# Four sizes of each expert projection, chosen at run time, in a linear-attention and hash-routing kernel

## The chip, the cores and the metric

The kernel runs on one core of one Trainium2 chip. The metric is the device time of one execution in microseconds (us). TensorE multiplies matrices, VectorE and ScalarE work on elements, GpSimd starts the gathers and scatters with indices, SyncE starts plain transfers.

## The reference

Linear attention with decay over 4 sequences of 768 positions and 8 heads of 64, and then a layer of experts: each of the 3,072 tokens goes to one of 8 experts by a hash of its id.

```python
expert_idx = token_ids * np.int64(2654435761) % np.int64(E)      # E = 8
for e in range(E):
    mask = expert_idx == e
    xe = x[mask]                          # x: [3072, 512], the attention's output
    h = np.maximum(xe @ w1[e], 0.0)       # w1[e]: [512, 1024]
    out[mask] = h @ w2[e]                 # w2[e]: [1024, 512]
```

All of it is in float32. The ids are random but fixed by a seed; the kernel doesn't know them when it is built, and computes the routing on the chip.

## The kernel before

It goes through 24 units of attention, each 128 positions of one sequence. Between them it computes the routing on VectorE: experts are ranked by their count of tokens, and the expert of rank w gets "window" w, with room for `CAPS[w]` tokens. Tokens that don't fit go to a loop at the end. The rows of a window are gathered, transposed, projected twice and scattered.

```python
EARLY = 19
CAPS = [376, 384, 392, 392, 400, 408, 416, 432]
PACE = 1400
ORDER = [0, 2, 3, 4, 5, 6, 7, 1]
...
        cap = route.tile([P, E], F32)          # capacity of each expert's window
...
        nc.vector.tensor_tensor(ee, iota_s[:, 0:E].unsqueeze(2).to_broadcast([P, E, E]),
                                win.unsqueeze(1).to_broadcast([P, E, E]), op=OP.is_equal)
        nc.vector.tensor_mul(ee, ee, iota_s[:, 0:E].unsqueeze(1).to_broadcast([P, E, E]))
        nc.vector.tensor_reduce(who_i[:], ee, axis=AX.X, op=OP.add)
...
        key_e = route.tile([P, E, NC], F32)    # tokens beyond the capacity are moved to the end
        nc.vector.tensor_tensor(key_e[:], cum, cap[:].unsqueeze(2).to_broadcast([P, E, NC]), op=OP.is_ge)
```

`yield n` in the routing says how much VectorE work a step is; after each attention unit, steps worth `PACE` are let through.

The projections of all but the first one use a scheme of seven products instead of eight for a 2x2 block matrix. The tokens of a window are split into two halves, the inner dimension and the outputs too. Sums of blocks are made on VectorE beforehand, and products are combined afterwards:

```python
    def quarters(x):
        K, M = x.shape[1] // 2, x.shape[2] // 2
        return [[x[:, j * K:(j + 1) * K, i * M:(i + 1) * M] for j in range(2)] for i in range(2)]

    def token_sums(x, name):
        a = quarters(x)
        ...
        todo = [lambda: nc.vector.tensor_add(s1, a[1][0], a[1][1]), lambda: nc.vector.tensor_sub(s2, s1, a[0][0]),
                lambda: nc.vector.tensor_sub(s3, a[0][0], a[1][0]), lambda: nc.vector.tensor_sub(s4, a[0][1], s2)]
        return [None, a[0][0], a[0][1], s4, a[1][1], s1, s2, s3], todo

    def seven(a, b, c, g, relu, todo):
        K, T = a[1].shape[1], a[1].shape[2]          # T: tokens of one half
        def product(i):
            ...
            for m in range(2):
                at = (2 * g + m) * P
                for k in range(K):
                    nc.tensor.matmul(ps[:, m, :], b[i][:, k, at:at + P], a[i][:, k, :],
                                     start=k == 0, stop=k == K - 1)          # L658
```

A first projection calls `seven` twice (K = 2), a second one once (K = 4), so each has 7 x 2 x 4 = 56 matmuls. A float32 matmul is two weight loads and two matmuls in the records, so a projection has 112 of each. The loop over the windows:

```python
    for n, e in enumerate(ORDER):
        then = ORDER[n + 1] if n + 1 < E else None
        ...
        if n == 0:
            flush(todo)
            eight(xTs[e], w1s[e], hT)                # the plain form, L718
        else:
            past = ORDER[n - 1]
            ...
            part = squares(past) // 2
            (both0, others0, _), (both1, others1, _) = (seven(a1, b1, quarters(hT[:]), g, True, todo) for g in range(2))
            others0(both0())
            turn_out(past, 0, part)                  # transpose and scatter of the window before
            others1(both1())
            turn_out(past, part, squares(past))
        a2, sums2 = token_sums(hT[:], f"h_{e}")
        ...
        flush(sums2)
        b1, todo = weight_sums(w1s[then], f"w1_{then}")
        todo.insert(2, lambda: turn(0, squares(then)))
        a1, more = token_sums(xTs[then], f"x_{then}")
        both, others, _ = seven(a2, b2, quarters(yT[:, :, 0:CAPS[e]]), 0, False, todo)
        others(both())
        flush(todo + more)
```

The only branches of the program are those of the loop over overflow tiles at the end.

Of the kernel before, what the change touches and what calls it, by code (L numbers as in the profile page):

```python
# [7 lines left out]
F32 = mybir.dt.float32  # L8
BF16 = mybir.dt.bfloat16
I32 = mybir.dt.int32  # L10
# [6 lines left out]
EARLY = 19  # L17
FIRST = 288

CAPS = [376, 384, 392, 392, 400, 408, 416, 432]  # L20
WBUFS = 3
UBUFS = 2
WARM = 10
PACE = 1400
W_AT = [20, 21, 22, 23]
ORDER = [0, 2, 3, 4, 5, 6, 7, 1]
SQ = 32
PACE_FIRST = 500

# [2 lines left out]
def kernel(  # L32
# [189 lines left out]
    q_dec = aconst.tile([P, HP, C], F32)  # L222
    ident = const.tile([P, P], F32)
    who_i = route.tile([P, E], I32)
    oend = route.tile([P, E], F32)
    ntot_i = route.tile([P, 1], I32)
    idx_all = route.tile([P, NTILE], I32)
# [32 lines left out]
    def routing():  # L260
# [48 lines left out]
        nc.vector.tensor_reduce(cap[:], ee, axis=AX.X, op=OP.add)  # L309
        yield 250  # L310

        nc.vector.tensor_tensor(ee, iota_s[:, 0:E].unsqueeze(2).to_broadcast([P, E, E]),
                                win.unsqueeze(1).to_broadcast([P, E, E]), op=OP.is_equal)
        yield 250
        nc.vector.tensor_mul(ee, ee, iota_s[:, 0:E].unsqueeze(1).to_broadcast([P, E, E]))
        yield 250
        with nc.allow_low_precision("sums of one number each, below 8"):
            nc.vector.tensor_reduce(who_i[:], ee, axis=AX.X, op=OP.add)
# [12 lines left out]

        nc.vector.tensor_add(cnt, cnt, gap[:])
        yield 200
        nc.vector.tensor_sub(cnt, cnt, cap[:])
        yield 200
        och_i = route.tile([P, E], I32)
# [22 lines left out]
        nc.vector.tensor_sub(shift, shift, cap[:])  # L359
        yield 200  # L360

        key_e = route.tile([P, E, NC], F32)
        nc.vector.tensor_tensor(key_e[:], cum, cap[:].unsqueeze(2).to_broadcast([P, E, NC]), op=OP.is_ge)
        yield 400
        nc.vector.tensor_mul(key_e[:], key_e[:], shift.unsqueeze(2).to_broadcast([P, E, NC]))
# [54 lines left out]
        nc.vector.tensor_scalar(x_rows[:].rearrange("p t k -> p k t"), list_ps[:], piece[:, 1:2], None, op0=OP.add)  # L420
        done.append("lists")
        yield 400

        b_i = route.tile([P, NTILE], I32)
        nc.vector.tensor_scalar(b_i[:], rc[:, 1], -1.0, None, op0=OP.add)
# [119 lines left out]

    w1s, w2s = {}, {}
    first_src = []

    def load_first(i):
        for part, at in enumerate(W_AT):  # L550
# [14 lines left out]
    for i, u in enumerate(units):  # L565
        if i + AHEAD < len(units):
            loads[units[i + AHEAD]] = load_qkv(*units[i + AHEAD])
        if i > 0:
            store_x(i - 1)
        if i == B:  # L570
            for b in range(0, NB, NB // 2):
                nc.sync.dma_start(
                    x_dram[0:DP * P, :].rearrange("(p b) q -> p b q", p=P)[:, b:b + NB // 2, :],
                    zeros[:].bitcast(F32).rearrange("p (b q) -> p b q", q=P))
        load_first(i)
        if i == 0:
            attention(*u, *ready.pop(u))
        if i + 1 < len(units):
            ready[units[i + 1]] = scores(*units[i + 1])
        if i > 0:  # L580
            attention(*u, *ready.pop(u))
        room = PACE if i >= B else PACE_FIRST
        while room > 0:
            room -= next(todo, TURN)
        if i >= EARLY:
            assert "lists" in done
            if i == EARLY:
                xT, gathers, turn = gather_window(0)
                xTs = {0: xT[:, :, 0:CAPS[0]]}
                early = gathers[:FIRST // SQ]  # L590
                del gathers[:FIRST // SQ]
            for _ in range(3):
                if early:
                    early.pop(0)()
            if i == len(units) - 2:
                turn(0, NB)
# [28 lines left out]
        return ([None, b[0][0], b[1][0], b[1][1], t4, t1, t2, t3],  # L625
                [lambda x=x: nc.vector.tensor_sub(*x) for x in todo])  # L626

    def quarters(x):
        K, M = x.shape[1] // 2, x.shape[2] // 2
        return [[x[:, j * K:(j + 1) * K, i * M:(i + 1) * M] for j in range(2)] for i in range(2)]  # L630

    def token_sums(x, name):
        a = quarters(x)
        K, M = x.shape[1] // 2, x.shape[2] // 2
        s = sums.tile([P, 3, K, M], F32, tag=f"s{K}", name=f"{name}_s")
        s1, s2, s4 = (s[:, i] for i in range(3))
        s3 = a[1][0]
        todo = [lambda: nc.vector.tensor_add(s1, a[1][0], a[1][1]), lambda: nc.vector.tensor_sub(s2, s1, a[0][0]),
                lambda: nc.vector.tensor_sub(s3, a[0][0], a[1][0]), lambda: nc.vector.tensor_sub(s4, a[0][1], s2)]  # L639
        return [None, a[0][0], a[0][1], s4, a[1][1], s1, s2, s3], todo  # L640

    def flush(todo):
        while todo:
            todo.pop(0)()

    def seven(a, b, c, g, relu, todo):

        K, T = a[1].shape[1], a[1].shape[2]  # L650

        def product(i):
            ps = psC.tile([P, 2, T], F32, tag="c", name=f"p{i}") if i in (5, 7) else psA.tile(
                [P, 2, T], F32, tag="a", name=f"p{i}")
# [5 lines that stand above are left out]
            return ps  # L660

        def one_more():
            if todo:
                todo.pop(0)()

        def done(i, j, ps, u):
            o = c[i][j][:, 2 * g:2 * g + 2, :]
            nc.vector.tensor_add(o, ps[:], u[:])  # L668
            if relu:
                nc.scalar.activation(o, o, AF.Relu)  # L670

        def both():

            u1 = sums.tile([P, 2, T], F32, tag="u1", bufs=UBUFS, name="u1")
            nc.scalar.copy(u1[:], product(1)[:])  # L675
            done(0, 0, product(2), u1)
            return u1

        def others(u1):
            u2, u3 = (sums.tile([P, 2, T], F32, tag=f"u{i}", bufs=UBUFS, name=f"u{i}") for i in (2, 3))  # L680
            p7 = product(7)
            one_more()
            p5 = product(5)
            one_more()
            if len(todo) > 2:
                one_more()
            nc.vector.tensor_add(u2[:], product(6)[:], u1[:])  # L687
            nc.vector.tensor_add(u3[:], p7[:], u2[:])
            done(1, 1, p5, u3)
            nc.vector.tensor_add(u2[:], p5[:], u2[:])  # L690
            one_more()
            done(1, 0, product(4), u3)
            one_more()
            done(0, 1, product(3), u2)

        def last(u1, then):

            u2, u3 = (sums.tile([P, 2, T], F32, tag=f"u{i}", bufs=UBUFS, name=f"u{i}") for i in (2, 3))
            p5 = product(5)
            nc.vector.tensor_add(u2[:], product(6)[:], u1[:])  # L700
            nc.vector.tensor_add(u3[:], p5[:], u2[:])
            done(0, 1, product(3), u3)
            nc.vector.tensor_add(u2[:], product(7)[:], u2[:])
            then()
            done(1, 1, p5, u2)
            done(1, 0, product(4), u2)

        return both, others, last
# [50 lines left out]
    def squares(e):  # L759
        return -(-CAPS[e] // SQ)  # L760
# [10 lines left out]
    for n, e in enumerate(ORDER):  # L771
        then = ORDER[n + 1] if n + 1 < E else None
        hT = sums.tile([P, FP, CAPS[e]], F32, tag="hT", name=f"hT_{e}")
        b2, todo = weight_sums(w2s[e], f"w2_{e}")
        if then is not None:
            xT, gathers, turn = gather_window(then)
            xTs[then] = xT[:, :, 0:CAPS[then]]
            flush(gathers)
        if n == 0:
            flush(todo)  # L780
            eight(xTs[e], w1s[e], hT)
        else:
            past = ORDER[n - 1]
            if then is None:

                nc.gpsimd.drain()
            part = squares(past) // 2
            (both0, others0, _), (both1, others1, _) = (seven(a1, b1, quarters(hT[:]), g, True, todo) for g in range(2))
            others0(both0())
            turn_out(past, 0, part)  # L790
            others1(both1())
            turn_out(past, part, squares(past))
        a2, sums2 = token_sums(hT[:], f"h_{e}")
        if then is None:
            flush(sums2)
            both, _, last = seven(a2, b2, quarters(yT[:, :, 0:CAPS[e]]), 0, False, [])
            whole = CAPS[e] // 2 // P
            last(both(), lambda: rows(e, range(whole)))
            rows(e, range(whole, NT))
            continue  # L800
        if then not in w1s:
            w1s[then] = load_window_w1(then)
        w2s[then] = load_window_w2(then)
        flush(sums2)
        b1, todo = weight_sums(w1s[then], f"w1_{then}")
        todo.insert(2, lambda: turn(0, squares(then)))
        a1, more = token_sums(xTs[then], f"x_{then}")
        both, others, _ = seven(a2, b2, quarters(yT[:, :, 0:CAPS[e]]), 0, False, todo)
        others(both())
        flush(todo + more)  # L810
    order.close()

    def overflow_tile(w1, w2, xT):
# [97 lines left out]
```

## Time and profile before

| | |
|---|---|
| time, median of 3 | 423.95 us (423.4 to 425.21) |
| span of the profiled execution | 516.1 us, mean TensorE clock 0.901 |
| TensorE busy (matmul, weight load) | 436.5 us, 406.4 us |
| VectorE, ScalarE, GpSimd busy | 308.5, 67.9, 259.0 us |
| moved by the DMA engines | 78.92 MB, mean 153 GB/s |

The profiled execution is slower than the timed ones. In the profile, PE is TensorE's matrix array and PEld its weight loads, DVE is VectorE, ACT ScalarE, POOL GpSimd and SP SyncE. PEclk is the clock that TensorE was granted, as a share of full speed or, in the rows of slices, in tenths of it. Lines of the kernel are written L658 for line 658. `<-` stands for "written from", and after "idle" it names what ended a wait. "issue" is idle time for which the profile shows no cause. Queue 8 and queue 14 of the DMA engines carry instructions.

### The profile page before, as it was taken

What the parts mean: (1) busy time and instruction counts of PE and PEld (TensorE: products, weight loads), DVE (VectorE), ACT (ScalarE), POOL (GpSimd) and SP (SyncE); (2) the same over time, 40 slices, a digit from 0 to 9 for tenths busy, and PEclk for the clock granted to TensorE, in tenths of its full rate; (3) what the DMA queues carried; (4) which work ended last, traced back from release to release, by engine and by line L of the source; (5) the groups of instructions that cost most, each with busy time, mean ns of one, the idle gap of its engine ahead of it and who ended that gap; (6) DMA issues with size and microseconds to landing.
All of it is one profiled execution on the core that took longest, in us unless ns stands there. A gap on an engine that the chain in (4) does not pass through costs nothing. (4 is left out here: it accounts for less than half of the span.)

```text
span 516.1 us, 8543 instructions
## 1 busy us (share of the span) xinstructions
PE 436.5 (85%) x3349; PEld 406.4 (79%) x3349; DVE 308.5 (60%) x492; ACT 67.9 (13%) x166; POOL 259.0 (50%) x266
## 2 busy tenths in 40 slices
PE   7998989779539999999839966999489948999993
PEld 4787878669429999999729935999389938999982
DVE  7887886534004777779346533774477437768821
ACT  1022332001001021021001100120012001201200
POOL 5454654437760018767752772067706760650552
PEclk9898999979757999999969955999879987999997
DMA  8899899975214035246141610424153414230011
GB/s 311 307 402 328 279 339 314 311 259 178 82 51 161 16 156 201 81 162 210 46 143 67 213 44 25 164 90 151 46 174 89 152 46 163 78 150 1 32 34 62
DMA packets 28105, 78.92 MB, mean 153 GB/s; under 512 B 4521, under 2 KB 6829, under 8 KB 25120
## 3 DMA queue, kind: packets, MB, share of 16 engines
q1 hardware_dynamic: 18160, 59.01, 32.5%
q0 software_dynamic: 6448, 13.06, 8.2%
q10 hardware_dynamic: 3456, 6.29, 3.3%
q8 instruction: 27, 0.44, 0.3%
q14 instruction: 14, 0.11, 0.1%
HBM read 65.50 MB, written 13.30 MB: 153 GB/s over the span
## 5 line engine op out<-in xcount | busy, mean ns | idle before, releaser
L753 POOL DMA_INDIRECT out_dram<-o_by,out_rows x91 | 100.1, 1100 | 157.0 <-DVE o_by L749 131.7
L538 POOL DMA_INDIRECT g<-x_pieces,x_rows x91 | 96.4, 1059 | 27.7 <-issue 26.2
L658 PE MATMUL p<-xT,w 128*128 128x196 f32 (+5 forms) x336 | 67.4, 352 | 29.7 <-DVE xT L639 22.8
L658 PEld LDWEIGHTS p<-xT,w 128*128 128x128 f32 x336 | 60.7, 200 | 33.7 <-DVE xT L639 24.7
L658 PE MATMUL p<-hT,w 128*128 128x196 f32 (+6 forms) x384 | 67.7, 336 | 0.1
L658 PEld LDWEIGHTS p<-hT,w 128*128 128x128 f32 x384 | 66.3, 193 | 0.3 <-issue 0.3
L658 PE MATMUL p<-h_s,w_t 128*128 128x196 f32 (+6 forms) x256 | 51.0, 349 | 6.8 <-issue 6.8
L658 PEld LDWEIGHTS p<-h_s,w_t 128*128 128x128 f32 x256 | 45.2, 198 | 11.2 <-issue 11.2
L687 DVE TENSOR_TENSOR u<-p,u 128x392 f32<-128x392 f32 (+6 forms) x21 | 12.1, 578 | 63.4 <-PE p L658 45.3
L668 DVE TENSOR_TENSOR yT<-p,u 128x392 f32<-128x392 f32 (+6 forms) x32 | 18.4, 574 | 51.0 <-remote 39.6
L718 PE MATMUL ps<-xT,w 128*128 128x128 f32 (+1 forms) x192 | 32.7, 319 | 16.3 <-issue 16.0
L718 PEld LDWEIGHTS ps<-xT,w 128*128 128x128 f32 x192 | 29.4, 228 | 19.6 <-issue 19.4
L670 ACT ACTIVATE hT<-hT 128x392 f32<-128x392 f32 (+5 forms) x56 | 30.1, 540 | 97.5 <-DVE hT L668 91.6
L658 PE MATMUL p<-x_s,w_t 128*128 128x196 f32 (+5 forms) x224 | 41.5, 339 | 0.0
L658 PEld LDWEIGHTS p<-x_s,w_t 128*128 128x128 f32 x224 | 39.9, 196 | 0.1
L626 DVE TENSOR_TENSOR w_t<-w,w_t 128x1024 f32<-128x1024 f32 x30 | 36.5, 1218 | 0.0
L675 ACT COPY u<-p 128x392 f32<-128x392 f32 (+6 forms) x22 | 10.7, 488 | 193.7 <-PE p L658 98.2
L473 DVE TENSOR_TENSOR sm<-sps,decay 128x512 f32<-128x512 f32 x48 | 30.8, 682 | 8.6 <-remote 4.3
L479 POOL TENSOR_TENSOR qd<-qkv,q_dec 128x512 f32<-128x512 f32 x17 | 21.6, 1271 | 26.7 <-DMA qkv<-in_qkv_dram 22.6
L467 PE MATMUL sps<-qkv 64*128 64x128 f32 x384 | 28.0, 285 | 7.6 <-DMA qkv<-in_qkv_dram 7.6
L668 DVE TENSOR_TENSOR hT<-p,u 128x392 f32<-128x392 f32 (+5 forms) x56 | 31.9, 575 | 4.2 <-ACT u L675 1.6
L467 PEld LDWEIGHTS sps<-qkv 64*128 64x128 f32 x384 | 23.4, 188 | 12.1 <-DMA qkv<-in_qkv_dram 9.1
(150 smaller groups left out, 585.1 us busy)
## 6 DMA issues: line engine op xcount, KB each, us to landing
w<-in_moe_w_dram SPq DMA_DIRECT2D x15, 2048.0 KB
qkv<-in_qkv_dram SPq DMA_DIRECT2D x23, 1024.0 KB
x_pieces<-turned ACTq DMA_DIRECT2D x24, 256.0 KB
w<-in_moe_w_dram SPq DMA_DIRECT2D x4, 512.0 KB
g<-x_pieces,x_rows POOLq DMA_INDIRECT x91
out_dram<-o_by,out_rows POOLq DMA_INDIRECT x91
qkv<-in_qkv_dram SPq DMA_DIRECT2D x2, 512.0 KB
x_pieces<-zeros SPq DMA_DIRECT2D x2, 128.0 KB
```

The source lines that it names most:

```text
L467: nc.tensor.matmul(sps[hd][:, hp, :], kT[half[hd], hp, :], qT[half[hd], hp, :], start=True, stop=True)
L473: nc.vector.tensor_mul(sm[:, hd], sps[hd][:], decay[:, hd])
L479: eng.tensor_tensor(qd[:], qT, q_dec[:], op=OP.mult)
L538: nc.gpsimd.indirect_dma_start(out=dst, out_offset=None, in_=x_dram[0:rows, :], in_offset=bass.IndirectOffsetOnAxis(ap=idx, axis=0), bound ...
L626: [lambda x=x: nc.vector.tensor_sub(*x) for x in todo])
L658: nc.tensor.matmul(ps[:, m, :], b[i][:, k, at:at + P], a[i][:, k, :], start=k == 0, stop=k == K - 1)
L668: nc.vector.tensor_add(o, ps[:], u[:])
L670: nc.scalar.activation(o, o, AF.Relu)
L675: nc.scalar.copy(u1[:], product(1)[:])
L687: nc.vector.tensor_add(u2[:], product(6)[:], u1[:])
L718: nc.tensor.matmul(ps[:, m, :], w[:, k, (f + m) * P:(f + m + 1) * P], x[:, k, ts], start=k == 0, stop=k == DP - 1)
L753: st = nc.gpsimd.indirect_dma_start(out=out_pieces, out_offset=bass.IndirectOffsetOnAxis(ap=out_rows[:, e * NT + t, k:k + 1], axis=0), in_ ...
```

## The change

For each of the windows 1 to 7 both projections are there four times, for half sizes of `CAPS/2`, `CAPS/2 - 4`, `CAPS/2 - 8` and `CAPS/2 - 12` tokens. All engines branch to the smallest that holds the expert's tokens. For this the tokens are dealt evenly to both halves: those from the middle of the expert's own count on are moved to the start of the second half. The aim is that TensorE doesn't multiply columns that hold no token. Window 0 keeps its one size.

```diff
-PACE = 1400
+PACE = 1500
+ARMS, STEP = 4, 4
+    arm_i = route.tile([P, E], I32)
...
+        size = route.tile([P, E], I32)
+        nc.vector.tensor_scalar(size[:], cnt, 1.0, None, op0=OP.add)
+        nc.vector.tensor_scalar(size[:], size[:], 1, None, op0=OP.logical_shift_right)
+        half_n = route.tile([P, E], F32)
+        nc.vector.scalar_tensor_tensor(half_n[:], cap[:], 0.5, size[:], op0=OP.mult, op1=OP.min)
+        move = route.tile([P, E], F32)
+        nc.gpsimd.tensor_scalar(move[:], cap[:], 0.5, None, op0=OP.mult)
+        nc.gpsimd.tensor_sub(move[:], move[:], half_n[:])
+        other = route.tile([P, E], F32)
+        nc.gpsimd.tensor_scalar(other[:], first[:], 0.0, None, op0=OP.is_equal)
+        nc.gpsimd.tensor_mul(move[:], move[:], other[:])
+        arm = route.tile([P, E], F32)
+        nc.gpsimd.tensor_scalar(arm[:], move[:], float((ARMS - 1) * STEP), None, op0=OP.min)
...
+        nc.vector.tensor_tensor(key_e[:], cum, half_n[:].unsqueeze(2).to_broadcast([P, E, NC]), op=OP.is_ge)
+        nc.vector.tensor_mul(key_e[:], key_e[:], move[:].unsqueeze(2).to_broadcast([P, E, NC]))
+        nc.vector.tensor_add(cum, cum, key_e[:])
...
+        nc.vector.tensor_mul(ee, by_win[:], arm[:].unsqueeze(1).to_broadcast([P, E, E]))
+        nc.vector.tensor_reduce(arm_i[:], ee, axis=AX.X, op=OP.add)
+        nc.vector.tensor_scalar(arm_i[:], arm_i[:], STEP.bit_length() - 1, None, op0=OP.logical_shift_right)
...
+        if i == EARLY + 1:
+            _, arms = nc.values_load_multi_w_load_instructions(
+                arm_i[0:1, :], min_val=0, max_val=ARMS - 1, ...)
+            arm_of.extend(arms)
...
-    def quarters(x):
+    def quarters(x, n=None):
         K, M = x.shape[1] // 2, x.shape[2] // 2
-        return [[x[:, j * K:(j + 1) * K, i * M:(i + 1) * M] for j in range(2)] for i in range(2)]
+        return [[x[:, j * K:(j + 1) * K, i * M:i * M + (n or M)] for j in range(2)] for i in range(2)]
+    def by_size(w, body):
+        def among(lo, hi):
+            if hi - lo == 1:
+                body(CAPS[w] // 2 - STEP * lo)
+                return
+            mid = (lo + hi) // 2
+            with tc.If(arm_of[w] < mid) as less:
+                among(lo, mid)
+            with less.Else():
+                among(mid, hi)
+        among(0, ARMS)
...
-            (both0, others0, _), (both1, others1, _) = (seven(a1, b1, quarters(hT[:]), g, True, todo) for g in range(2))
-            others0(both0())
-            turn_out(past, 0, part)
-            others1(both1())
-            turn_out(past, part, squares(past))
+            def up(size):
+                rest = list(todo)
+                (both0, others0, _), (both1, others1, _) = (
+                    seven(some(a1, size), b1, quarters(hT[:], size), g, True, rest) for g in range(2))
+                others0(both0())
+                turn_out(past, 0, part)
+                others1(both1())
+                turn_out(past, part, squares(past))
+            by_size(e, up)
...
-        both, others, _ = seven(a2, b2, quarters(yT[:, :, 0:CAPS[e]]), 0, False, todo)
-        others(both())
-        flush(todo + more)
+        def down(size):
+            flush(sums2(size))
+            rest = todo + more()
+            both, others, _ = seven(some(a2, size), b2, quarters(yT[:, :, 0:CAPS[e]], size), 0, False, rest)
+            others(both())
+            flush(rest)
+        if n == 0:
+            down(CAPS[e] // 2)
+        else:
+            by_size(e, down)
```

`some(a, n)` cuts all operands to n tokens, and `token_sums` now makes its sums for n tokens. The second projection of the last window has the four sizes in the same way. The four arms stand one after the other in each engine's program; an arm begins behind two compares with a branch, and ends with a jump to behind the last arm. TensorE's part of one arm is 112 weight loads, 112 matmuls and some four more instructions.

More of the change, by code (lines that the diff above doesn't have):

```diff
@@ L310, in routing @@
         yield 250
-        nc.vector.tensor_tensor(ee, iota_s[:, 0:E].unsqueeze(2).to_broadcast([P, E, E]),
+        by_win = route.tile([P, E, E], F32)
+        nc.vector.tensor_tensor(by_win[:], iota_s[:, 0:E].unsqueeze(2).to_broadcast([P, E, E]),
                                 win.unsqueeze(1).to_broadcast([P, E, E]), op=OP.is_equal)
         yield 250
-        nc.vector.tensor_mul(ee, ee, iota_s[:, 0:E].unsqueeze(1).to_broadcast([P, E, E]))
+        nc.vector.tensor_mul(ee, by_win[:], iota_s[:, 0:E].unsqueeze(1).to_broadcast([P, E, E]))
         yield 250
@@ L333, in routing @@
         yield 200
+        size = route.tile([P, E], I32)
+        nc.vector.tensor_scalar(size[:], cnt, 1.0, None, op0=OP.add)
+        yield 200
+        nc.vector.tensor_scalar(size[:], size[:], 1, None, op0=OP.logical_shift_right)
+        yield 200
+        half_n = route.tile([P, E], F32)
[6 more added lines that the diff above has]
+        nc.gpsimd.tensor_mul(move[:], move[:], other[:])
+        yield 400
+        arm = route.tile([P, E], F32)
+        nc.gpsimd.tensor_scalar(arm[:], move[:], float((ARMS - 1) * STEP), None, op0=OP.min)
         nc.vector.tensor_sub(cnt, cnt, cap[:])
@@ L362, in routing @@
         key_e = route.tile([P, E, NC], F32)
+        nc.vector.tensor_tensor(key_e[:], cum, half_n[:].unsqueeze(2).to_broadcast([P, E, NC]), op=OP.is_ge)
+        yield 400
+        nc.vector.tensor_mul(key_e[:], key_e[:], move[:].unsqueeze(2).to_broadcast([P, E, NC]))
+        yield 400
+        nc.vector.tensor_add(cum, cum, key_e[:])
+        yield 400
         nc.vector.tensor_tensor(key_e[:], cum, cap[:].unsqueeze(2).to_broadcast([P, E, NC]), op=OP.is_ge)
@@ L422, in routing @@
         yield 400
+        nc.vector.tensor_mul(ee, by_win[:], arm[:].unsqueeze(1).to_broadcast([P, E, E]))
+        yield 250
+        with nc.allow_low_precision("sums of one number each, below 2 ** 8"):
+            nc.vector.tensor_reduce(arm_i[:], ee, axis=AX.X, op=OP.add)
+        yield 250
+        nc.vector.tensor_scalar(arm_i[:], arm_i[:], STEP.bit_length() - 1, None, op0=OP.logical_shift_right)
+        done.append("sizes")
+        yield 250
         b_i = route.tile([P, NTILE], I32)
@@ L547 @@
     first_src = []
+    arm_of = []
     def load_first(i):
@@ L584 @@
             room -= next(todo, TURN)
+        if i == EARLY + 1:
+            assert "sizes" in done
+            _, arms = nc.values_load_multi_w_load_instructions(
+                arm_i[0:1, :], min_val=0, max_val=ARMS - 1, skip_runtime_bounds_check_because="clamped to these")
+            arm_of.extend(arms)
         if i >= EARLY:
@@ L626, in weight_sums, with some @@
                 [lambda x=x: nc.vector.tensor_sub(*x) for x in todo])
-    def quarters(x):
+    def quarters(x, n=None):
         K, M = x.shape[1] // 2, x.shape[2] // 2
-        return [[x[:, j * K:(j + 1) * K, i * M:(i + 1) * M] for j in range(2)] for i in range(2)]
+        return [[x[:, j * K:(j + 1) * K, i * M:i * M + (n or M)] for j in range(2)] for i in range(2)]
+    def some(a, n):
+        return [x if x is None else x[:, :, 0:n] for x in a]
+    def by_size(w, body):
[9 more added lines that the diff above has]
+        among(0, ARMS)
     def token_sums(x, name):
@@ L637, in token_sums, with todo @@
         s3 = a[1][0]
-        todo = [lambda: nc.vector.tensor_add(s1, a[1][0], a[1][1]), lambda: nc.vector.tensor_sub(s2, s1, a[0][0]),
-                lambda: nc.vector.tensor_sub(s3, a[0][0], a[1][0]), lambda: nc.vector.tensor_sub(s4, a[0][1], s2)]
-        return [None, a[0][0], a[0][1], s4, a[1][1], s1, s2, s3], todo
+        of = [None, a[0][0], a[0][1], s4, a[1][1], s1, s2, s3]
+        def todo(n=M):
+            x, y, z, u = (some(v, n) for v in (a[0], a[1], (s1, s2), (s3, s4)))
+            return [lambda: nc.vector.tensor_add(z[0], y[0], y[1]), lambda: nc.vector.tensor_sub(z[1], z[0], x[0]),
+                    lambda: nc.vector.tensor_sub(u[0], x[0], y[0]), lambda: nc.vector.tensor_sub(u[1], x[1], z[1])]
+        return of, todo
     def flush(todo):
@@ L787 @@
             part = squares(past) // 2
-            (both0, others0, _), (both1, others1, _) = (seven(a1, b1, quarters(hT[:]), g, True, todo) for g in range(2))
-            others0(both0())
-            turn_out(past, 0, part)
-            others1(both1())
-            turn_out(past, part, squares(past))
+            def up(size):
[6 more added lines that the diff above has]
+                turn_out(past, part, squares(past))
+                assert not rest
+            by_size(e, up)
         a2, sums2 = token_sums(hT[:], f"h_{e}")
         if then is None:
-            flush(sums2)
-            both, _, last = seven(a2, b2, quarters(yT[:, :, 0:CAPS[e]]), 0, False, [])
             whole = CAPS[e] // 2 // P
-            last(both(), lambda: rows(e, range(whole)))
-            rows(e, range(whole, NT))
+            def down(size):
+                flush(sums2(size))
+                both, _, last = seven(some(a2, size), b2, quarters(yT[:, :, 0:CAPS[e]], size), 0, False, [])
+                last(both(), lambda: rows(e, range(whole)))
+                rows(e, range(whole, NT))
+            by_size(e, down)
             continue
@@ L803 @@
         w2s[then] = load_window_w2(then)
-        flush(sums2)
         b1, todo = weight_sums(w1s[then], f"w1_{then}")
@@ L807, with down @@
         a1, more = token_sums(xTs[then], f"x_{then}")
-        both, others, _ = seven(a2, b2, quarters(yT[:, :, 0:CAPS[e]]), 0, False, todo)
-        others(both())
-        flush(todo + more)
+        def down(size):
+            flush(sums2(size))
+            rest = todo + more()
[5 more added lines that the diff above has]
+        else:
+            by_size(e, down)
     order.close()
```

## The prediction

> **What bounds the kernel now.** I read the page's busy shares first, then the table of stretches, then TensorE's timeline, and last the parts that tell of instruction fetch and branches.
>
> ```profile
> PE 436.5 (85%) x3349; PEld 406.4 (79%) x3349; DVE 308.5 (60%) x492; ACT 67.9 (13%) x166; POOL 259.0 (50%) x266
> PEclk9898999979757999999969955999879987999997
> ```
>
> TensorE is busy for 85% of the span, VectorE for 60%. The profiled execution took 516 us, the timed ones 424, so the profile must not be read as if it were the timed run. Its clock row has slices at 5 to 7. The stretches show where the difference lies (attention, first projection of the first expert, all other projections, tail; columns as in the header):
>
> ```profile
> core 0: us, PE busy (x) PEld busy (x) DVE busy (x) ACT busy (x) POOL busy (x), PEclk, DMA share, GB/s
> 0.00:110.70 110.70, 96.66 (x1466) 79.93 (x1466) 82.25 (x193) 22.08 (x74) 56.26 (x77) 0.95 0.92 327
> 110.70:159.20 48.50, 32.23 (x194) 29.27 (x192) 6.79 (x7) 4.07 (x11) 30.13 (x30) 0.71 0.29 95
> 159.20:505.80 346.60, 306.28 (x1686) 296.38 (x1685) 218.25 (x290) 41.15 (x80) 170.64 (x157) 0.92 0.32 108
> 505.80:516.10 10.30, 1.31 (x10) 0.86 (x8) 1.25 (x2) 0.58 (x1) 1.97 (x2) 0.70 0.21 77
> ```
>
> ```profile
> 176.00:250.00 74.00, 73.95 (x447) 73.65 (x447) 56.82 (x76) 11.12 (x22) 44.53 (x39) 1.00 0.43 146
> 295.00:318.00 23.00, 13.46 (x33) 8.25 (x33) 5.49 (x6) 0.00 (x0) 15.02 (x15) 0.57 0.15 44
> ```
>
> From 176 to 250 us TensorE has no gap: 73.95 of 74 us at clock 1.00. From 295 to 318 us it issues 33 matmuls where 136 of 200 columns would fit. Four such stretches, and the one from 128 to 156 us, make the profile long. How long is a matmul in a clean stretch? From TensorE's timeline (start, length, instructions):
>
> ```profile
> 178.36 4.14 PE L658 MATMUL p<-xT,w 128*128 128x196 f32 x24
> 182.34 2.82 PE L658 MATMUL p<-x_s,w_t 128*128 128x196 f32 x16
> ...
> 395.09 8.60 PE L658 MATMUL p<-hT,w 128*128 128x208 f32 x48
> 403.53 5.79 PE L658 MATMUL p<-h_s,w_t 128*128 128x208 f32 x32
> ```
>
> From start to start, 24 matmuls of 196 columns take 3.98 us, 165.8 ns each, and 48 of 208 columns 8.44 us, 175.8 ns each: 12 columns cost 10.0 ns, so 0.833 ns a column, and 165.8 - 163.3 = 2.5 ns fixed. The eight second projections and seven first ones have 112 matmul records each. With half of each capacity as the column count (188, 192, 196, 196, 200, 204, 208, 216, together 1,600; without the first 1,412) that is 112 x 3,012 x 0.833 ns + 1,680 x 2.5 ns = 281.1 + 4.2 = 285 us. The 192 records of the first projection at 128 columns (109 ns by the same rule) are 21 us. So: attention 110.7 + 21 + 285 + tail 10.3 = 427 us, against 424 timed. The timed kernel therefore has TensorE busy nearly without pause from 111 us to the tail, and what counts is columns on TensorE plus any pause put into its stream.
>
> [...]
>
> ```profile
> q8 instruction: 27, 0.44, 0.3%
> q14 instruction: 14, 0.11, 0.1%
> ```
>
> [...] By their times one comes each time TensorE passes a further 256 instructions, about every 20 us in the projections; one takes 0.88 to 1.25 us there. The other engines fetch 8 KB at a time. [...] The loop at the end has such branches (minimum, median, maximum in ns):
>
> ```profile
> L836 PEldq COMPARE_BRANCH  x3: 101/187/304, 507.5 to 513.6; - x3
> L836 DVEq COMPARE_BRANCH  x3: 41/51/56, 508.1 to 513.5; - x3
> L836 ACTq COMPARE_BRANCH  x3: 38/38/50, 508.4 to 513.2; - x3
> ```
>
> TensorE's are 0.10 to 0.30 us[...].
>
> **The change part by part.** (a) Columns. The token ids are fixed by the seed: the experts hold 345, 377, 386, 388, 388, 389, 393 and 406 tokens, in windows of 376, 384, 392, 392, 400, 408, 416 and 432. Dealt evenly, the halves of windows 1 to 7 are 189, 193, 194, 194, 195, 197, 203 against half capacities 192, 196, 196, 200, 204, 208, 216. The surplus is 3, 3, 2, 6, 9, 11, 13; in steps of 4, at most 12, the arms drop 0, 0, 0, 4, 8, 8 and 12 columns: 32 in all. Each column is saved by 112 records in the first and 112 in the second projection: 224 x 32 x 0.833 ns = **5.97 us** off TensorE, on the path. VectorE's and ScalarE's operations shrink too, by some 2%, beside it.
>
> (b) Routing. VectorE gets three operations of 192 elements (0.33 to 0.37 us each by the present ones of that form) and six small ones (0.13 to 0.23 us), 2.2 us; GpSimd five small ones. The attention stage has VectorE busy 82 of 111 us while the DMA engines are at 0.92 share, and 100 more units of routing are let through per step, so I count 0 to 0.5 us.
>
> (c) Loading the sizes. Each engine loads eight numbers into registers once, after attention unit 20; a load of one by SyncE took 0.27 to 0.54 us. TensorE's sequencer must wait for VectorE there. TensorE has slack at that point (16.8 of 21 us busy from 85 to 106 us). 0 to 1 us.
>
> (d) Branches. There are 14 places, and at each an engine executes two compares and one jump. On TensorE, 0.10 to 0.30 us each, some 0.6 us. This is hidden if its sequencer is ahead of the array: the waits that the sequencer executes itself are recorded 16 to 17 matmuls, hence about 2.7 us, before the array reaches their place. So 0 by itself.
>
> (e) Fetch. One arm is 112 weight loads, 112 matmuls and some four more instructions, 228, or 0.89 of a block. Four arms are 3.6 blocks. Arm 0 is entered by falling through and left over three arms (2.7 blocks); arm 3 the other way round; each place has one jump of 1.8 blocks or more. If the target is present, that costs nothing. If it must be fetched, a fetch begins about 0.65 us after its cause (the last branch of TensorE against the packet that follows it) and lasts 0.9 to 1.25 us: 1.6 to 1.9 us alone, longer beside a weight load. With the 0.6 us of branches that takes nearly all of the 2.7 us lead; a second block or a busy queue lets TensorE run dry by 1 to 2 us, 14 times: 14 to 28 us.
>
> Sum without misses: 424.0 - 6.0 + 1 = 419. Sum with exposed misses: 433 to 447.
>
> **The rivals.** *One: the misses are exposed.* For it: [...] fetches in the attention stage that begin up to 140 instructions late, so the fetch can queue behind data. Against it: [...] the lead of 2.7 us. It makes 433 to 447. *Two: VectorE takes over.* Its own branches are cheap and its four arms (27 to 30 instructions each) are about one of its blocks, so it should not miss; but it is busy 57 of 74 us in the clean stretch, and a late sum holds TensorE's first product. That would give back a few of the 6 us: 421 to 425. *Three: the gain is larger,* because shorter operations also shorten pauses at the projections' borders. The bottom-up sum leaves no pauses of that size, so I see at most 8 us: 416.
>
> **Range and chances.** I give the case without exposed misses a little over half and take 420 us, slightly above its 419, as the middle of everything. The range of 415.5 to 438 holds that case whole and the lower half of the other. Faster by 2% means below 415.5, 8.5 us against a saving of 6: 0.06. Slower by 2% means above 432.4, which is most of rival one: 0.25. Between them 0.69.
>
> **What would show it.** Right: in the profile after, matmuls of the projections with 204, 200, 196 and 192 columns at 0.833 ns a column; no TensorE gap at the borders of projections; stretches between borders shorter by 112 x 0.833 ns a column. Instruction packets on queue 8 should rise by 3 x 14 x 0.89 = 37 if everything skipped is fetched too, to about 64, and stay near 30 if the arms are jumped over. Wrong: pauses of 1 us or more before the first matmul of a projection, with an instruction packet just ahead of it and the releaser "issue"; or pauses that end with a VectorE sum. The prediction fails outright if each border costs more than 1.5 us.

## The result, and the profile after

The changed kernel takes 483.74 us (median; 481.91 to 485.13), the kernel before 423.89 us beside it: a ratio of 1.140, with the interval [1.135, 1.145]. It is 60 us slower, where 420 us were predicted.

The page of the changed kernel (busy time and clock row, then the queues that carry instructions):

```profile
PE 415.6 (86%) x3349; PEld 396.4 (82%) x3349; DVE 308.5 (64%) x501; ACT 66.8 (14%) x166; POOL 262.5 (54%) x271
PEclk9999999989999999979896988998989889799996
...
q8 instruction: 62, 1.02, 0.9%
q14 instruction: 32, 0.26, 0.2%
```

TensorE executes the same 3,349 products as before, but there are 62 instruction packets on its queue 8, and the clock row falls to 6, 7 or 8 in nine of the twenty slices of the second half. The stretches show where the time went: attention with the first projection of the first expert, all other projections, and the tail.

```profile
core 0: us, PE busy (x) PEld busy (x) DVE busy (x) ACT busy (x) POOL busy (x), PEclk, DMA share, GB/s
0.00:126.00 126.00, 114.46 (x1657) 99.24 (x1658) 91.08 (x209) 25.72 (x85) 70.31 (x95) 0.99 0.88 314
126.00:471.50 345.50, 300.00 (x1686) 296.34 (x1685) 216.12 (x290) 40.52 (x80) 190.19 (x175) 0.93 0.35 114
471.50:483.40 11.90, 1.13 (x9) 0.86 (x8) 1.25 (x2) 0.58 (x1) 1.97 (x2) 0.64 0.18 66
```

The profile of the kernel before that the prediction used was of a slow execution (516 us), and all timed runs of the first batch of experiments (e1 to e4) were slow as well, the kernel before among them (481 to 539 us), so that no time of that batch is compared. I therefore took another profile of the kernel before, with a span of 422.5 us (h1_before_again, below). Its stretch of the projections, same columns:

```profile
126.30:412.40 286.10, 286.06 (x1687) 285.74 (x1685) 218.22 (x291) 41.16 (x80) 199.55 (x175) 1.00 0.41 135
```

So the projections went from 286.1 us, without a pause, to 345.5 us with TensorE idle for 45.5 and the clock at 0.93. The stretch ahead of them is 0.3 us shorter and the tail 1.8 us longer: the 61 us between the two spans are all but 1.5 us in the projections. (The longest branch of the overflow loop in the tail takes 3.0 us here and 0.3 us in the kernel before.)

What holds TensorE there? First, the branches of the changed kernel, on four of the five engines (count, then minimum, median and maximum in ns, then the first and last start in us; the unconditional jumps at the end of an arm are recorded under the same name):

```profile
L685 ACTq COMPARE_BRANCH  x40: 34/38/50, 128.8 to 473.3; - x40
L685 PEldq COMPARE_BRANCH  x40: 65/300/6304, 141.0 to 472.3; - x40
L685 POOLq COMPARE_BRANCH  x40: 34/38/50, 141.1 to 474.2; - x40
L685 DVEq COMPARE_BRANCH  x40: 43/47/63, 145.7 to 472.9; - x40
```

No branch of the other engines lasts over 63 ns (SyncE's, not shown, 34 to 57). On TensorE 18 of 40 last between 3.3 and 6.3 us, 75.8 us in all; the other 22 last 0.07 to 0.32 us. The median hides this: read the maximum. The wait for an instruction block doesn't appear as a wait here; it is inside the duration of the branch (in the 3.79 us of the jump below lies its packet of 1.4 us). TensorE's timeline has 12 pauses in the stage, 45.5 us in all, and puts four down to "issue" and eight to an operation of VectorE, as in these two:

```profile
183.10 4.22 PE L723 MATMUL p<-xT,w 128*128 128x196 f32 x24 [1.12 <-DVE x_s L702]
410.87 11.40 PE L723 MATMUL p<-hT,w 128*128 128x204 f32 x48 [4.32 <-DVE h_s L702]
```

But 11 of the 12 pauses end 0.16 to 0.49 us after the end of a branch of 3.3 us or more, whichever name they carry (the jumps ahead of these two end at 182.61 and 410.70 us). The twelfth, at 208.16 us, is taken up in the last section.

One jump in full: at the end of the first projection of one expert TensorE leaves arm 0 over three arms. The jump begins at 198.78 us and lasts 3.79 us (largest of the three in the first line; the second line is queue 8 in the stretch 198.7 to 202.7 us, one packet, with its share of 16 engines):

```profile
L685 PEldq COMPARE_BRANCH  x3: 65/77/3790, 198.8 to 202.8; - x3
```
```profile
q8 instruction: 1, 0.02, 2.2%
```

2.2% of 16 x 4.0 us is a packet of 1.4 us. It begins between 199.7 and 199.9 us, so about 1.0 us after the begin of the jump, and ends by about 201.2; the jump is over at 202.57. The wait is thus 1.0 us until the packet, 1.4 us of packet, and another 1.4 us until TensorE goes on.

What the array sees is shown by TensorE's timeline, of the changed kernel and then of the kernel before, at the border of a first and a second projection with the same 196 columns (of two different experts; start, length, instructions, in brackets the idle time ahead):

```profile
250.26 1.49 PE L723 MATMUL p<-xT,w_t 128*128 128x196 f32 x8
251.59 1.49 PE L723 MATMUL p<-x_s,w 128*128 128x196 f32 x8
260.51 11.16 PE L723 MATMUL p<-hT,w 128*128 128x196 f32 x48 [7.43 <-issue]
```

```profile
198.66 1.49 PE L658 MATMUL p<-x_s,w 128*128 128x196 f32 x8
199.99 8.12 PE L658 MATMUL p<-hT,w 128*128 128x196 f32 x48
```

Before, the second projection follows the first without a gap, and its first 48 products take 8.12 us. After, there is a pause of 7.43 us, and 48 products of the same size take 11.16 us. Here two fetches stand in a row: the sequencer leaves the first projection's arm with a jump of 3.89 us, and 0.2 us after its end, behind one compare that doesn't jump, a branch begins that lasts 6.30 us. The stretch in which the clock was lowered:

```profile
256.30:266.54 10.24, 6.03 (x19) 6.06 (x20) 2.05 (x3) 0.38 (x1) 7.80 (x9) 0.50 0.62 217
```

The granted clock is 0.50 for 10.24 us, and TensorE is busy for 6.03 us of them: that costs the 3.0 us by which the 48 products are slower. The stretch begins 3.2 us after the start of the pause and lasts until 6.0 us after its end. The changed kernel has eight such stretches in its projections, from 3.41 to 10.24 us long. Each begins 3.1 to 4.7 us after the start of a pause of 2.41 us or more; the other four of the 12 pauses (0.56, 1.12, 1.15 and 2.55 us) have none. The sum of the eight (length, then the busy time of each engine):

```profile
sum 47.78, PE 34.95 PEld 35.05 DVE 7.76 ACT 1.85 POOL 25.53; mean PE 4.37 PEld 4.38 DVE 0.97 ACT 0.23 POOL 3.19
```

The 6.03 us of work above lost 3.0 us, half of it. At the same rate 34.95 us of work at clock 0.50 lose 17.5 us, which is my estimate of what the clock costs beside the 45.5 us of pauses. The kernel before has no such stretch in its projections (clock 1.00 in the row above).

### The rule for the waits

I counted the instructions of TensorE in the built program and set each branch against blocks of 256 instructions. That size is an estimate: in the first profile of the kernel before, queue 8 has 27 packets of 16,384 bytes for 6,804 recorded instructions of TensorE, 252 per packet. One reading fits all 40 branches of the changed kernel: they last as if TensorE had two blocks at hand, the one it executes and the next. With the same position of the block borders it also fits the 132 branches of f1, f4, g1, g2 and g3 (below).

| Jump | Duration | Cases in the changed kernel |
|---|---|---|
| not taken, or into the next block when that is loaded | 0.07 to 0.32 us | 22 |
| two blocks ahead or more, no jump shortly before it | 3.3 to 3.9 us | 9 |
| just behind another jump, to a block that isn't loaded yet (also the next one) | 3.4 to 6.3 us, six of them 4.8 and more | 9 |

Which blocks are loaded is worked out from the count; no view shows it. The long ones in the last row fit a load that the jump before had begun and that must end first: in the wait of 4.96 us that begins at 307.54 us queue 8 has two packets, which begin 0.7 and 1.1 us into it. Three more of the six waits of 4.8 us and more have two packets. The other two, of 6.30 and 5.34 us, have one, which begins only 4.0 and 2.9 us into the wait; what they wait for until then isn't shown.

An arm is 0.89 of a block. Arm 0 is left over three arms: one wait. From arm 3 on the way in, two jumps stand in a row: over two arms, and then at once over one more. On the other engines an executed arm has at most 31 recorded instructions (GpSimd; VectorE 29, ScalarE 12), so four have at most some 124. That is about one packet of queue 14: in the first profile of the kernel before it has 14 packets of 8,192 bytes for 1,739 recorded instructions of the other four engines, 124 per packet. Their branches don't wait (63 ns at most).

### The profile page after: what moved, and what is told of

Same layout as the page of the kernel before. It is cut to its first block, busy times and chain, and to the rows that moved or that the text cites. A ratio compares the mean times of both kernels' runs of the same rounds, so it can differ in the third digit from the quotient of the medians.

```text
span 483.4 us, 8776 instructions
## 1 busy us (share of the span) xinstructions
PE 415.6 (86%) x3349; PEld 396.4 (82%) x3349; DVE 308.5 (64%) x501; ACT 66.8 (14%) x166; POOL 262.5 (54%) x271
## 4 chain that ended last, share of the span: by engine, by line
PE 41%; issue 30%; POOL 14%; DMA 8%; DVE 5%; POOLq 1%; DVEq 0%; SPq 0%
PE p L723 25%; POOL out_dram L818 7%; POOL g L574 6%; DMA qkv<-in_qkv_dram 6%; PE ps L783 5%; PE sps L503 4%; PE xps L549 3%; PE xps L528 3%; PE kv L536 2%; DMA out_dram<-o_by,out_rows 1%; DMA scratch<-x_pieces,x_rows 1%; DVE h_s L702 1%; DVE sm L509 1%; POOL out_dram L799 0%; DVE x_s L702 0%
## 5 line engine op out<-in xcount | busy, mean ns | idle before, releaser
L723 PE MATMUL p<-hT,w 128*128 128x196 f32 (+4 forms) x384 | 75.1, 361 | 24.9 <-DVE h_s L702 9.5
L723 PE MATMUL p<-xT,w 128*128 128x196 f32 (+3 forms) x336 | 66.5, 360 | 20.6 <-issue 17.1
L733 DVE TENSOR_TENSOR hT<-p,u 128x392 f32<-128x392 f32 (+3 forms) x56 | 31.3, 565 | 31.3 <-PE p L723 30.0
L733 DVE TENSOR_TENSOR yT<-p,u 128x392 f32<-128x392 f32 (+4 forms) x32 | 18.1, 565 | 44.3 <-PE p L723 44.0
L723 PE MATMUL p<-h_s,w_t 128*128 128x196 f32 (+4 forms) x256 | 43.8, 329 | 0.0
L735 ACT ACTIVATE hT<-hT 128x392 f32<-128x392 f32 (+3 forms) x56 | 29.6, 532 | 96.2 <-DVE hT L733 96.2
L723 PE MATMUL p<-x_s,w_t 128*128 128x196 f32 (+3 forms) x224 | 39.6, 330 | 0.0
L752 DVE TENSOR_TENSOR u<-p,u 128x392 f32<-128x392 f32 (+4 forms) x21 | 11.9, 568 | 43.3 <-PE p L723 43.3
L515 POOL TENSOR_TENSOR qd<-qkv,q_dec 128x512 f32<-128x512 f32 x17 | 21.6, 1270 | 20.4 <-DMA qkv<-in_qkv_dram 17.5
L549 PE MATMUL xps<-sm,qkv 128*64 128x128 f32 x384 | 26.2, 275 | 1.7 <-DVE sm L509 1.7
L518 POOL TENSOR_TENSOR kd<-qkv,k_dec 128x512 f32<-128x512 f32 x20 | 21.8, 1088 | 9.5 <-DMA qkv<-in_qkv_dram 5.9
```

The source lines that it names most:

```text
L515: eng.tensor_tensor(qd[:], qT, q_dec[:], op=OP.mult)
L518: eng.tensor_tensor(kd[:], kn, k_dec[:].unsqueeze(2).to_broadcast([P, H, Dh]), op=OP.mult)
L549: nc.tensor.matmul(xps[half[hd], hp, :], vt[:, 2 * hp + hd, :], sm[:, hd, hp, :], start=(c == 0 and hp == 0), stop=(hp == HP - 1))
```

## The experiments

The theories: **fetch** (jumps beyond the next block wait in TensorE's sequencer), **columns** (another number of columns, or uneven operand shapes, makes products slower), **routing** (the added routing and the loading of sizes cost the time), **VectorE** (its sums come later and hold TensorE). Stage below is the time from the first product of the projections to the last; the kernel before has 285.6 us there from the start of the first product to the start of the last. The rows of stretches are of that stage and have the columns given above.

### One size, no branch: e1_one_size, f3_one_size

The halves are dealt evenly, sizes are loaded into registers, but each projection is there once, at full size.

```diff
-ARMS, STEP = 4, 4
+ARMS, STEP = 1, 4
```

> One size, so no branch anywhere; routing, dealing and loading of the sizes stay. Theory A (TensorE's sequencer waits for instruction blocks after its jumps): 424 to 426 us. Rival B (the added routing and the register loads cost the time): 475 to 484. Rival C (branches cost by making all engines wait for each other at each border, whatever the distance): also 424 to 426, so this run separates B alone.

> One size and no branch, routing and register loads kept, once more beside an undisturbed kernel before. Theory A: 424 to 426 us. Rival B (routing and register loads): 475 to 484.

e1: 531.76 us, first batch. f3: 427.24 us, ratio 1.006 [1.002, 1.011], a little above the 424 to 426 expected. Its projections are as before, with no pause:

```profile
132.30:418.40 286.10, 286.01 (x1687) 285.69 (x1685) 218.10 (x291) 41.17 (x80) 198.76 (x174) 1.00 0.40 135
```

So routing and the register loads are no cause of 60 us. They cost 0.2 to 1.1%, which is 1 to 4.5 us. I could not place that more closely: in the profiles the projections begin anywhere from 124.7 to 132.4 us.

### Known sizes, no branch: e2_sizes_known, f2_sizes_known

The sizes that the experts of this seed need are written into the program. It computes the routing as the change does, but it isn't a general kernel.

```diff
+KNOWN = [0, 0, 0, 0, 1, 2, 2, 3]
...
-        among(0, ARMS)
+        body(CAPS[w] // 2 - STEP * KNOWN[w])
```

> No branch; the sizes that the ids of this input need (half sizes less 0, 0, 0, 4, 8, 8, 12) are written into the program. Theory A and rival C: the whole saving of columns, 32 x 224 x 0.833 ns = 6.0 us, without its price: 417 to 420 us. If the saving itself is an illusion (rival D: VectorE holds TensorE at the borders): 423 to 425.

> The sizes known beforehand and no branch, once more beside an undisturbed kernel before: the saving of columns alone. Theory A: 417 to 420 us. Rival D (VectorE holds TensorE at the borders): 423 to 425.

e2: 543.43 us, first batch. f2: 418.01 us, ratio 0.985 [0.979, 0.991].

```profile
124.70:404.60 279.90, 279.90 (x1686) 279.61 (x1684) 216.09 (x290) 40.57 (x80) 194.90 (x175) 1.00 0.41 138
```

The stage is 6.0 us shorter, and TensorE is busy for all of it. The columns bring what they were to bring, and they and VectorE's work with four sizes do no harm. The columns theory and the VectorE theory fall.

### Four arms, all of full size: e3_four_same

```diff
-                body(CAPS[w] // 2 - STEP * lo)
+                body(CAPS[w] // 2)
```

> Four arms and all branches as in the change, but every arm computes the full half size, so nothing is saved. Theory A: the price alone, 484 + 6 = 488 to 492 us. Rival E (sizes that differ from window to window are what slows it): 424 to 430.

562.50 us, first batch; but the branches can be read:

```profile
L685 PEldq COMPARE_BRANCH  x40: 65/300/5496, 172.4 to 548.7; - x40
```

18 long ones again, 71.2 us in sum beside 75.8 of the change. The waits need the arms, not the sizes.

### Two arms instead of four: e4_two_arms_8, f1_two_arms_8

Two arms of 0.89 of a block each: the one jump of a place then leads into the next block.

```diff
-ARMS, STEP = 4, 4
+ARMS, STEP = 2, 8
```

> Two sizes 8 columns apart instead of four 4 apart; as many places, one compare instead of two. An arm is 0.89 of a block of 256 instructions, so every jump now ends in the next block, which is as a rule already there. Theory A: saving 24 x 224 x 0.833 ns = 4.5 us, a few waits of 1 to 3 us where a border was crossed just before: 419 to 427 us. Rival C (each place costs some 4.5 us whatever the distance): 475 to 485.

> The two sizes 8 columns apart once more, beside a kernel before that runs near its 424 us. Theory A (only a jump past the next block waits): 24 columns saved, 4.5 us, one or two waits of 2 us partly hidden by the sequencer's lead: 419 to 424 us. Rival C (each place costs the same 4.5 us whatever the distance): 475 to 485.

e4: 544.88 us, first batch; one of its 22 branches lasted over 0.35 us. f1: 422.75 us, ratio 0.995 [0.992, 0.998].

```profile
L685 PEldq COMPARE_BRANCH  x22: 65/281/1182, 140.3 to 407.6; - x22
```

```profile
125.20:406.80 281.60, 281.58 (x1687) 281.26 (x1685) 216.55 (x290) 40.72 (x80) 197.29 (x176) 1.00 0.41 138
```

With half the arms the waits don't halve, they vanish: the longest is 1.2 us, which TensorE's lead of 2.7 us hides. The stage is without a pause and 4.5 us shorter than before, which is what 24 columns are worth. This experiment decides for the fetch theory: runtime branches in the same 14 places, even dealing and register loads are all still there, and the jumps no longer lead beyond the next block. A place also has one compare instead of two now; that isn't the cause, as a compare that doesn't jump takes 65 to 99 ns in f4 below.

### Four arms of full size, always arm 0, or always arm 3: f4_same_arm0, g2_same_arm3

```diff
-        nc.gpsimd.tensor_scalar(arm[:], move[:], float((ARMS - 1) * STEP), None, op0=OP.min)
+        nc.gpsimd.memset(arm[:], float(0 * STEP))
...
-                body(CAPS[w] // 2 - STEP * lo)
+                body(CAPS[w] // 2)
```

g2 has `3 * STEP` there. Both multiply full halves, and differ from each other only in the way through the jumps.

> Four arms that all compute the full half size, and arm 0 always taken. Each place has then one jump, over three arms (2.7 blocks), and no other that leaves its block. Theory A: in the profile one wait of 3.3 to 3.9 us at each of the 14 places and none on the compares, 1 to 2 us of each beyond the sequencer's lead, and a few more where the next block is entered just behind the jump: 440 to 465 us, well below the 484 of the change, whose other arms need two fetches. Rival C (the price belongs to the place, not to the jump): 488 to 492.

> Four arms of the full half size, arm 3 always taken. Each place then has a compare that jumps 1.8 blocks and right behind it one that jumps 0.9, and no jump at the end. Theory A with two fetches in a row: 8 to 10 us of waiting at each place, less 2.7 us of lead, and a colder clock behind it: 510 to 545 us. Theory A with one fetch in each place, whatever the arm: 454, as with arm 0. Rival C: 454 too.

f4, one far jump per place: 454.18 us, ratio 1.072 [1.068, 1.076].

```profile
L685 PEldq COMPARE_BRANCH  x42: 65/77/3952, 140.6 to 442.1; - x42
```

```profile
125.50:441.30 315.80, 294.42 (x1687) 289.73 (x1686) 218.07 (x290) 41.17 (x80) 193.64 (x176) 0.98 0.38 125
```

14 long waits in 14 places, 51.4 us; 15 pauses, 21.4 us, or 1.5 us per place.

g2, two jumps in a row per place: 506.30 us, ratio 1.194 [1.187, 1.201], somewhat below what I had expected.

```profile
L685 PEldq COMPARE_BRANCH  x28: 238/3391/4530, 146.0 to 467.3; - x28
```

```profile
131.00:491.30 360.30, 312.39 (x1686) 306.40 (x1685) 218.08 (x290) 41.17 (x80) 190.40 (x174) 0.93 0.33 109
```

24 of 28 branches are long, 84.1 us; the four short ones are those for which the count of blocks gives a target at hand. The pauses are 47.9 us. With the same columns the way through the arms alone makes 52 us of difference. Also, f4 never takes an arm but the first: the far jump over arms that aren't executed is enough to cost 27 us beside f3, which has the same columns and routing.

### Four sizes in the second projection alone: g3_down_only

```diff
-            by_size(e, up)
+            up(CAPS[e] // 2)
```

> The four sizes for the second projections alone; the first ones have one size and no branch. Half the places, 3 us saved: theory A: 445 to 462 us. If the price came once (routing, first use of a branch): 475 or more.

434.29 us, ratio 1.022 [1.016, 1.028]: less than I had expected (445 to 462 us).

```profile
L685 PEldq COMPARE_BRANCH  x20: 65/262/3882, 163.6 to 422.0; - x20
```

```profile
130.00:421.20 291.20, 284.50 (x1687) 282.48 (x1685) 217.18 (x290) 41.14 (x80) 194.86 (x175) 1.00 0.40 133
```

8 long waits, 28.0 us in sum, but only 6.7 us of pauses, in six places: five of 0.3 to 0.9 us behind a single wait of 3.2 to 3.9 us, and one of 3.6 us where arm 3 has two in a row. The granted clock stays at 1.00. I had scaled the loss with the number of branch places. It doesn't scale so: with a projection without branches between two places, the exit of one place isn't followed at once by the entry of the next, and most waits stand alone. TensorE's lead takes nearly all of such a wait. That the projection in between gives the next block time to load is argued, not measured.

### Two sizes, a step of its own per window: g1_two_arms_own

As two arms, but the smaller size of a window is 4, 8 or 12 below its full one, so all 32 columns are saved.

```diff
-ARMS, STEP = 4, 4
+STEPS = [0, 4, 4, 4, 4, 8, 8, 12]
...
-        nc.vector.tensor_scalar(arm_i[:], arm_i[:], STEP.bit_length() - 1, None, op0=OP.logical_shift_right)
+        nc.vector.tensor_tensor(arm_i[:], move_w[:], steps[:], op=OP.is_ge)
...
-        among(0, ARMS)
+        with tc.If(arm_of[w] < 1) as less:
+            body(CAPS[w] // 2)
+        with less.Else():
+            body(CAPS[w] // 2 - STEPS[w])
```

> Two sizes for each window, with a step of its own (4, 4, 4, 4, 8, 8 and 12 columns for windows 1 to 7): all 32 columns saved, all jumps to the next block. Theory A: 1.5 us below the two sizes 8 apart, so 419 to 422 us and faster than both kernels. If each place has a price whatever the distance: 475 or more.

422.07 us, ratio 0.994 [0.991, 0.997].

```profile
L681 PEldq COMPARE_BRANCH  x20: 65/281/3002, 146.3 to 412.7; - x20
```

```profile
131.20:411.90 280.70, 280.29 (x1687) 279.70 (x1685) 216.18 (x290) 40.53 (x80) 191.38 (x173) 1.00 0.41 138
```

The stage is 280.3 us, one wait of 3.0 us is left. It beats both kernels, the one before by 0.3 to 0.9%, and isn't told apart from f1, though 1.5 us less than f1 had been expected.

### The kernel before, once more: h1_before_again

No edit.

> The kernel before once more, for a profile near its timed 424 us, to compare stages. From the column count: 285 us from the first product of the seven-product scheme to the end of the last, no TensorE pause over 0.9 us between them, and a span of 415 to 425 us. If the stretches in which TensorE issued only every few hundred ns belong to the kernel and not to that one execution, they will be there again and the span will be near 516.

424.21 us, beside 426.26 us for another run of the same kernel; its stretch is shown with the result.

## Why the prediction was wrong, point by point

**The bound and (a), columns: right.** The stage was worked out at 285 us and measured at 285.6 us. The saving of 5.97 us is 6.0 us in f2.

**(b) and (c), routing and loading: possibly too small.** Together 0 to 1.5 us were allowed; f3 gives 1 to 4.5 us. Of a loss of 60 us this explains little.

**(d), branches: right.** On other engines they cost 34 to 63 ns; on TensorE up to 0.34 us where the target is at hand. The lead of 2.7 us exists as well: in the changed kernel a single wait of about 3.8 us leaves a pause of 1.1 to 1.2 us (at 183.10 and 452.66 us).

**(e), fetch: the step that failed.** Three of its terms were wrong.

- *The length of one.* "1.6 to 1.9 us alone" was the time until the packet ends. Measured are 3.3 to 3.9 us. The packet begins 0.9 to 1.0 us after the begin of the jump (once 1.6), not 0.65, and the term left out is the 1.3 to 1.5 us from the packet's end until TensorE goes on. I looked at the packets and took their end for the end of the wait. In the trace of the kernel before no far jump of TensorE was there to check it with, and the text should have said so.
- *Their number.* One fetch per place was counted. Arms 1 to 3 have two jumps each, and the jumps of neighbouring places follow each other at once: 9 of the 18 waits stand just behind another jump and last 3.4 to 6.3 us. With arm 3 everywhere 14 places give 24 long branches; with arm 0 everywhere 14.
- *What a pause brings with it.* The sum has no term for the clock. The stage after is 345.2 us = 279.6 us of products without branches (f2) + 45.5 of pauses + 17.5 of halved clock (above) + 2.6 that stay unexplained.

So a place costs 3.3 us of pause on average and 1.3 us of clock, where the text had 1 to 2 us in all. With 14 to 28 us the case of exposed misses came to 433 to 447 us. With 63 us of pauses and clock, less the 6 us of columns, it is 481 us; the unexplained 2.6 us make up nearly all of the rest.

**The chances.** The case without exposed misses got "a little over half". It rested on the lead of 2.7 us, which is there but too short, and on blocks further ahead being present, which no trace had shown. The range up to 438 us held about a third of the other case's 433 to 447, not its lower half. The 27 packets of the kernel before, one for each block passed, couldn't tell whether a target two or three blocks ahead is at hand. The far jumps measured since, of 3.3 us and more, speak against it.

**The rivals.** One was right in kind and 37 us short in size. Two falls, though eight pauses carry VectorE's name: f2 has the same VectorE work in the stage (216.09 us beside 216.12) and no pause. Three falls: no border of the kernel before had a pause to be shortened.

**What would show it.** Pauses ahead of a projection's first product, as the text said, though only four of them with the releaser "issue"; and over 1.5 us per border, 45.5 for 14. The count of packets agrees by chance: 62, near the "about 64 if everything skipped is fetched too". But f4, which skips just as many arms, has 57, and two arms have 40. So the count alone doesn't say which blocks were fetched or when.

## What to carry to other kernels

In these runs a choice between program parts was cheap on TensorE as long as every jump landed in the block being executed or in the next one: two arms of fewer than 256 instructions each, and no second jump close behind the first (f1: the longest branch 1.2 us, no pause). Before writing arms, count TensorE's instructions per arm, loads and products both, and hold the distance against the block of 256 estimated above; here two arms per place gave a ratio of 0.994 (g1) and four 1.140, for the same 32 columns. For the wait look at the longest branch on TensorE's sequencer, since the median and the list of waits hide it (here 6.3 us beside a median of 0.3).

## What had not been expected of the hardware

- A far jump of TensorE took 3.3 to 3.9 us in the changed kernel, of which the packet itself is 0.9 to 1.5 us; 1.3 to 1.5 us pass after it.
- A jump or a plain crossing into the next block waited too where it came right behind a far jump: in the changed kernel at 202.8 us TensorE stood still until 208.05 us, with the packet at about 205.7 us. By the count of instructions the jump ahead of it had landed some eight instructions before the end of a block. In f4 the three pauses over 3 us (of 15) follow jumps that landed some 8, 10 and 44 instructions before the end of one.
- The price of a wait went with its distance from the next: pauses of 0.8 us per long wait in g3 (places apart), 1.5 us in f4 (one per place), 3.4 us per place in g2 (two in a row).
- A pause of 7.4 us made the next 48 products 3.0 us slower; the clock was at half for 10.24 us, of which 6.0 lay behind the pause.

It stays open how the routing's cost of 1 to 4.5 us divides, and what makes the last 2.6 us of the stage.
